# A decode block on one core: head 27's rows of wo by eight small loads on partitions 0 to 63, LN2's sums on the vector engine, one filler product fewer

## The chip, the core and the metric

The kernel runs on one core of a Trainium2 chip, as one program from the first load to the last store. The metric is the device time of one execution in microseconds (us). Beside the timed runs there is one profiled execution; its span is the time between its first and its last instruction, and its own time is a little longer. All profile lines come from that execution, and times in them count from the start of its span.

## What is computed

One decode step (one new token, batch 2) of a transformer block with adaptive layer norm: attention over the last 4096 positions of a key and a value cache (32 query heads on 8 key-value heads, head size 128), then a feed-forward block with SiLU. Everything is float32. The model size D is 512 and the hidden size F is 1792.

```
mod = silu(c) @ w_mod                      # six vectors per batch row
h   = layernorm(x) * (1 + ca) + sa
o   = softmax(q k^T / sqrt(128)) v         # q = h @ wq, last 4096 keys and values
x   = x + ga * (o @ wo)                    # wo: 4096 x 512, 32 heads of 128 rows
h   = layernorm(x) * (1 + cb) + sb         # LN2
x   = x + gb * (silu(h @ w1) @ w2)
```

The inputs are 97.5 MB, of which the keys and values are 67 MB, wo is 8 MB, w1 and w2 are 3.7 MB each.

## The kernel before

**Loads.** All weights and caches go through one buffer of eight slots of 16 KB on each of the 128 partitions (`slots`, RING = 8), filled in turn (`stream`, L72). SP issues these loads in program order: w_mod, x, wq, then keys and values of four groups in turn (`load_group`, L79), then wo, w1 and w2 (`load_runs`, L85). SP is one queue of instructions: a load that has to wait holds back all that SP issues later. wo comes in two loads (`load_wo`, L359): heads 0 to 23 in slots 0 to 2 and heads 24 to 31 in slot 3. Both are issued as soon as the last group's scores are done with the key slots, about 10 us before their data can move, since the last values stand ahead of them in the DMA queues. w1 follows in two loads, w2 in five.

**Semaphores.** Each load that SP or ACT issues reports its landing on one of eight semaphores, DMAHW0 to DMAHW7, which the program gives out in turn: the load of c, from ACT, has 0, x has 1, wq 2, the first keys 3, the first values 4, and so on; the fourth values have 2, wo's heads 0 to 23 have 3, and heads 24 to 31 have 4. A load that takes a semaphore for a second time gets a wait for the load that had it last, unless SP has waited for that one already.

**Work.** Four groups (batch row times half of the heads) run one after the other. Each has scores on TensorE (`scores`, L274), a softmax (`softmax`, L290), the weighted sum of the values (`weighted`, L319), and a turn of the result by products with a small identity (`collect`, L335: four products `oT`, L345, each of which gives 128 x 4, and a copy into `oTn`, L353, where a head q has the 32 columns `oTn[:, q, :]`).

**The tail.** After the last group TensorE multiplies `oTn` of each head with its rows of wo (`acc_o`, L413: 32 products), ACT and TensorE turn that sum (`gather`, L392), DVE adds the residual (`x1T`), and LN2 runs with its columns on partitions: `column_means` (L439) sums over partitions by four products with the matrix `mean512` for the mean, and again by four for the variance, between the second and the third quarter of the product with w1 (`hid`, L459). Then SiLU, the product with w2 (`acc_yw`, L489, and `yx`, L501), a last DVE step (L522) and the store (L523).

**Fillers.** `busy(n, ...)` (L263) issues n products whose result nothing reads; there are four of them ahead of the 32 products with wo.

In float32 each product of the program is two passes of TensorE, so the profile counts twice as many matmuls as the text here.

Of the kernel before, what the change touches and what calls it, by code (L numbers as in the profile page):

```python
# [8 lines left out]
F32 = mybir.dt.float32  # L9
AF = mybir.ActivationFunctionType  # L10
ALU = mybir.AluOpType
AX = mybir.AxisListType

P = 128
B, D = 2, 512
HQ, HKV, DH = 32, 8, 128
G = HQ // HKV
F = 1792
EPS = 1e-5
RING = 8  # L20


def first_load(slots):
# [5 lines left out]
def adaln_block(  # L29
# [4 lines left out]
    v_cache: bass.AP,  # L34
    wq: bass.AP,
    wo: bass.AP,
    w1: bass.AP,
    w2: bass.AP,
    c: bass.AP,
# [13 lines left out]
    nc = tc.nc  # L53
# [5 lines left out]
    once = ctx.enter_context(tc.tile_pool(name="once", bufs=1))  # L59
# [25 lines left out]
    def load_runs(w, per, lo, hi):  # L85

        e = w.shape[1]
        n = -(-(hi - lo) * e // 4096)
        t = stream(n)[:, : (hi - lo) * e].rearrange("p (q e) -> p q e", e=e)
        inorder(nc.sync.dma_start(t, w.rearrange("(p q) e -> p q e", q=per)[:, lo:hi, :]))  # L90
        return t
# [23 lines left out]
    mean512 = const([P, P], "mean512")  # L115
# [19 lines left out]
    qs = const([P, 4 * 256 + 64], "qs")  # L135
    nc.gpsimd.memset(qs, 0.0)  # L136
    rowsum = const([P, 4], "rowsum")

    oTn = const([P, 32, 32], "oTn")
    nc.gpsimd.memset(oTn, 0.0)  # L140
    hT, uT = const([P, 4, 32], "hT_b"), const([P, F // P, 32], "uT")
    nc.gpsimd.memset(hT, 0.0)
# [8 lines left out]
    inorder = tc.keep_in_program_order  # L151
# [106 lines left out]
    vt = {0: load_group(v_cache, 0)}  # L258
    stat = lambda grp, v, s: qs[:, 256 * grp + 64 * v + 32 * s : 256 * grp + 64 * v + 32 * s + 32]

    oT = bank("O", "oT")[:, :64]
    STEPS = 4
    def busy(n, unread):  # L263

        for _ in range(n):
            inorder(nc.tensor.matmul(  # L266
                unread[0:32, :],
                id4,
                warm,
                start=True,  # L270
                stop=True,
            ))
# [62 lines left out]
    def collect(grp, o_ps, rl):  # L335

        o_sb = once.tile([P, 4 * DH], F32, tag="wide", name=f"ob{grp}")
        for c in (slice(0, D // 2), slice(D // 2, D)):
            nc.scalar.activation(o_sb[:, c], o_ps[:, c], AF.Copy, scale=rl)  # L339
        last = grp == STEPS - 1  # L340
        if last:
            busy(1, junk[0])
        cols = oT[:, 16 * grp : 16 * grp + 16]
        for v in range(4):
            inorder(nc.tensor.matmul(  # L345
                cols[:, 4 * v : 4 * v + 4],
                o_sb[:, v * DH : (v + 1) * DH],
                id4[:, 4 * v : 4 * v + 4],
                start=True,
                stop=True,  # L350
            ))
        b, n = divmod(grp, 2)
        (nc.vector.tensor_copy if last else nc.scalar.copy)(  # L353
            oTn[:, 16 * n : 16 * n + 16, 16 * b], cols
        )

    wot, junk = [], []

    def load_wo(lo, hi):  # L359
        wt = load_runs(wo, 32, lo, hi)  # L360
        wot.extend(wt[:, q, :] for q in range(hi - lo))

    for grp in range(STEPS):
        s_ps = scores(grp)
        if grp < STEPS - 1:
            kt[grp + 1] = load_group(k_cache, grp + 1)
        else:
            load_wo(0, 24)
            load_wo(24, 32)
        rl = softmax(grp, s_ps)  # L370
        o_ps = weighted(grp)
        if grp == STEPS - 1:
            junk.append(bank("C", "junk0"))
        if grp < STEPS - 1:
            vt[grp + 1] = load_group(v_cache, grp + 1)
        collect(grp, o_ps, rl)
# [30 lines left out]

    acc = bank("D", "acc_o")
    ao = bank("A", "ao")[:, :P]
    busy(4, junk[0])  # L410
    for q in range(32):
        g = q % 4
        inorder(nc.tensor.matmul(  # L413
            acc[32 * g : 32 * g + 32, :],
            oTn[:, q, :],
            wot[q],
            start=(q < 4),
            stop=(q >= 28),
        ))
    gather(ao, acc, "acc_o_sb", True, True, fill=1)  # L420
    busy(1, junk[1])
# [16 lines left out]

    def column_means(t, name):  # L439

        m = bank("B", name)[:, :B]
        for k in range(4):
            inorder(nc.tensor.matmul(m, mean512, t[:, k, :], start=(k == 0), stop=(k == 3)))
        return m

    mean = column_means(x1T, "mean_b")
    busy(1, junk[1])
    dT = once.tile([P, 4, B], F32, tag="dT", name="dT")
    nc.vector.tensor_sub(dT, x1T, mean[:, None, :].to_broadcast([P, 4, B]))
# [2 lines left out]
    )  # L452
    sq = once.tile([P, 4, B], F32, tag="sq", name="sq")
    nc.vector.tensor_mul(sq, dT, dT)
    FC = F // 4
    hp = bank("A", "hid")[:, :FC]
    for k in range(4):
        for g in range(4):
            inorder(nc.tensor.matmul(  # L459
                hp[32 * g : 32 * g + 32, :],  # L460
                hT[:, k, :],
                w1t[k][:, g * FC : (g + 1) * FC],
                start=(k == 0),
                stop=(k == 3),
            ))
        if k == 1:
            var = column_means(sq, "var_b")
            std = once.tile([P, B], F32, tag="stdb", name="std_b")
            nc.scalar.activation(std, var, AF.Sqrt, bias=eps_t)
            rstd = once.tile([P, B], F32, tag="rstdb", name="rstd_b")  # L470
            nc.vector.reciprocal(rstd, std)
# [53 lines left out]
    tc.no_tile_sem_insts.add(store.ins.name)  # L525


_INS = ["A_x", "A_k_cache", "A_v_cache", "A_wq", "A_wo", "B_w1", "B_w2", "c", "w_mod"]


# [59 lines left out]
```

## Time and profile before

| | |
|---|---|
| time, median of 3 runs | 233.1 us (233.04 to 233.44) |
| the profiled execution: its own time, its span | 233.04 us, 231.4 us |
| TensorE (PE) busy | 126.8 us (55%) |
| PE weight loads (PEld) | 45.9 us (20%) |
| VectorE (DVE), ScalarE (ACT), GpSimd (POOL) busy | 15.0, 19.7, 7.7 us |
| granted TensorE clock, mean | 0.80 |
| moved by DMA | 97.65 MB, 422 GB/s over the span |

A line of the profile's groups names the program line, the engine, the operation and the tiles (out<-in). SPq is SP's queue; "DMA slots<-in_A_wo_dram" is the landing of a load of wo into the slots. A chain of waits lists what the last instruction waited for, followed back to the start. In the rows of the stages, "(x20)" counts instructions and PEclk is the granted clock of TensorE, 1.00 for full speed. w1 and w2 are named in_B_w in the trace, since numbers in names are left out.

### The profile page before, as it was taken

The numbers are of one execution on the slowest core, as the hardware profiler recorded it, in microseconds if no ns is written. First come the engines' busy times: TensorE is split into PE (matmuls) and PEld (weight loads), VectorE is DVE, ScalarE is ACT, GpSimd is POOL, SyncE is SP. The second block draws the span as 40 slices with busy tenths as digits, with TensorE's granted clock in tenths as the row PEclk, the third lists the DMA queues.
The fourth block names the chain that finished last, engine by engine and source line by source line (L and its number), as shares of the span: only waits on it lengthen the run. The fifth ranks groups of instructions, "written<-read, shape, count | busy, mean of one in ns | idle before, by whom it ended". The sixth has DMA issues, their size and how long they took to land.

```text
span 231.4 us, 2188 instructions
## 1 busy us (share of the span) xinstructions
PE 126.8 (55%) x982; PEld 45.9 (20%) x982; DVE 15.0 (6%) x44; ACT 19.7 (9%) x45; POOL 7.7 (3%) x28
## 2 busy tenths in 40 slices
PE   0005906831950781491096078139509607999986
PEld 0003301310210221121033012112202202345333
DVE  0004020000011000002000000100000200000130
ACT  0203010110040010001001000100100100000331
POOL 8102000000000000000000000000000000000000
PEclk9999995985796596598579659656957965999999
DMA  9998988989889898898999989999899999999993
GB/s 399 417 454 362 544 362 385 513 374 532 362 374 532 374 513 374 385 513 385 487 396 396 510 385 467 408 408 498 385 430 445 419 456 408 416 405 442 413 411 137
DMA packets 2915, 97.65 MB, mean 422 GB/s; under 512 B 460, under 2 KB 476, under 8 KB 1116
## 3 DMA queue, kind: packets, MB, share of 16 engines
q1 hardware_dynamic: 2748, 97.52, 97.9%
q8 instruction: 7, 0.11, 0.2%
q10 hardware_dynamic: 160, 0.01, 0.0%
HBM read 97.53 MB, written 0.01 MB: 421 GB/s over the span
## 4 chain that ended last, share of the span: by engine, by line
DMA 73%; PE 23%; POOL 2%; issue 1%; SPq 0%; ACT 0%; DVE 0%; POOLq 0%
DMA slots<-in_A_v_cache_dram 50%; PE o L326 16%; DMA slots<-in_A_wq_dram 13%; DMA slots<-in_B_w_dram 10%; PE q L235 4%; PE acc_yw L489 1%; PE yx L501 1%; PE qT L245 0%; POOL qs L136 0%; POOL oTn L140 0%; SPq L152 0%; ACT q_sb L243 0%; POOL warm L114 0%; POOL avg L104 0%; POOL same L108 0%
## 5 line engine op out<-in xcount | busy, mean ns | idle before, releaser
L326 PE MATMUL o<-slots,probs 128*32 128x512 f32 x256 | 37.9, 755 | 29.1 <-DMA slots<-in_A_v_cache_dram 29.1
L281 PE MATMUL s<-slots,qs 128*32 128x512 f32 x256 | 35.5, 718 | 32.3 <-DMA slots<-in_A_k_cache_dram 32.3
L326 PEld LDWEIGHTS o<-slots,probs 128*32 128x32 f32 x256 | 11.5, 131 | 52.2 <-issue 52.2
L281 PEld LDWEIGHTS s<-slots,qs 128*32 128x32 f32 x256 | 9.4, 130 | 55.2 <-issue 39.0
L235 PE MATMUL q<-slots,hq_T 128*32 128x512 f32 x64 | 9.2, 724 | 7.3 <-DMA slots<-in_A_wq_dram 7.3
L293 DVE TENSOR_REDUCE mx<-s 128x1 f32<-128x512 f32 x4 | 2.8, 691 | 140.5 <-PE s L281 140.5
L173 PE MATMUL mean_a<-mv_a,avg 128*128 128x1 f32 x2 | 0.6, 347 | 18.4 <-DVE mv_a L170 18.4
L266 PE MATMUL junk<-warm,id 128*32 128x512 f32 x20 | 9.6, 595 | 0.0
L339 ACT ACTIVATE ob<-o,rl 128x256 f32<-128x256 f32 x8 | 3.4, 470 | 69.4 <-PE o L326 69.4
L413 PE MATMUL acc_o<-slots,oTn 128*32 128x512 f32 x64 | 7.2, 593 | 0.0
L295 ACT ACTIVATE mp<-part,mx 128x8 f32<-128x8 f32 x4 | 1.2, 300 | 70.0 <-DVE mx L293 70.0
L209 PE MATMUL m_sp<-slots,scT 128*32 128x512 f32 x32 | 5.9, 827 | 0.0
L345 PE MATMUL oT<-id,ob 128*128 128x4 f32 x32 | 4.2, 255 | 1.9 <-ACT ob L339 1.9
L235 PEld LDWEIGHTS q<-slots,hq_T 128*32 128x32 f32 x64 | 2.3, 130 | 13.3 <-issue 13.2
L345 PEld LDWEIGHTS oT<-id,ob 128*128 128x128 f32 x32 | 3.9, 191 | 5.5 <-ACT ob L339 5.5
L308 PE MATMUL lp<-rowsum,same 128*128 128x1 f32 x8 | 1.7, 286 | 5.1 <-ACT pr L303 5.1
L206 PE MATMUL m_a<-slots,scT 128*32 128x256 f32 x32 | 3.6, 543 | 1.1 <-POOL scT L163 1.1
L413 PEld LDWEIGHTS acc_o<-slots,oTn 128*32 128x32 f32 x64 | 3.6, 110 | 3.3 <-issue 3.1
L173 PEld LDWEIGHTS mean_a<-mv_a,avg 128*128 128x128 f32 x2 | 0.5, 310 | 18.4 <-issue 18.4
L297 PE MATMUL mg<-mp,same 128*128 128x8 f32 x8 | 1.6, 266 | 4.6 <-ACT mp L295 4.6
L459 PE MATMUL hid<-slots,hT_b 128*32 128x448 f32 x32 | 3.4, 544 | 0.0
L489 PE MATMUL acc_yw<-slots,uT 128*32 128x512 f32 x22 | 2.8, 599 | 0.9 <-DMA slots<-in_B_w_dram 0.9
(95 smaller groups left out, 59.9 us busy)
## 6 DMA issues: line engine op xcount, KB each, us to landing
slots<-in_w_mod_dram SPq DMA_DIRECT2D x1, 6144.0 KB, 17.1
slots<-in_A_wo_dram SPq DMA_DIRECT2D x1, 6144.0 KB, 25.6
slots<-in_B_w_dram SPq DMA_DIRECT2D x1, 2688.0 KB, 17.8
slots<-in_A_wo_dram SPq DMA_DIRECT2D x1, 2048.0 KB, 29.6
slots<-in_B_w_dram SPq DMA_DIRECT2D x1, 2048.0 KB, 23.1
slots<-in_B_w_dram SPq DMA_DIRECT2D x1, 896.0 KB, 19.6
slots<-in_B_w_dram SPq DMA_DIRECT2D x1, 768.0 KB
slots<-in_B_w_dram SPq DMA_DIRECT2D x3, 256.0 KB, 16.0
```

The source lines that it names most:

```text
L206: nc.tensor.matmul(m_a[r, :], scT[:, k, :], ab[:, g], start=(k == 0), stop=(k == 3))
L209: nc.tensor.matmul(m_sp[r, :], scT[:, k, :], cd[:, g], start=(k == 0), stop=(k == 3))
L235: inorder(nc.tensor.matmul(q_ps[32 * g : 32 * g + 32, :], hq_T[:, k, :], wqt[:, k, lo : lo + 4 * DH], start=(k == 0), stop=(k == 3),))
L266: inorder(nc.tensor.matmul(unread[0:32, :], id4, warm, start=True, stop=True,))
L281: inorder(nc.tensor.matmul(s_ps[32 * c : 32 * c + 32, :], stat(grp, v, s), kt[grp][:, lo : lo + 512], start=(s == 0 and v == 0), stop=(s = ...
L293: nc.vector.tensor_reduce(mx, s_ps, axis=AX.X, op=ALU.max)
L326: inorder(nc.tensor.matmul(o_ps[r : r + 32, :], probs[grp % 2][:, 32 * n + 16 * s : 32 * n + 16 * s + 32], vt[grp][:, lo : lo + 512], star ...
L339: nc.scalar.activation(o_sb[:, c], o_ps[:, c], AF.Copy, scale=rl)
L345: inorder(nc.tensor.matmul(cols[:, 4 * v : 4 * v + 4], o_sb[:, v * DH : (v + 1) * DH], id4[:, 4 * v : 4 * v + 4], start=True, stop=True,))
L413: inorder(nc.tensor.matmul(acc[32 * g : 32 * g + 32, :], oTn[:, q, :], wot[q], start=(q < 4), stop=(q >= 28),))
L459: inorder(nc.tensor.matmul(hp[32 * g : 32 * g + 32, :], hT[:, k, :], w1t[k][:, g * FC : (g + 1) * FC], start=(k == 0), stop=(k == 3),))
L489: inorder(nc.tensor.matmul(yw[32 * g : 32 * g + 32, :], uT[:, tt, :], w2t[tt], start=(tt < 4), stop=(tt >= WIDE - 4),))
```

## The change

Head 27's rows of wo no longer come with the other heads. On the host wo is packed as 31 heads, and head 27's 128 rows of 512 are packed as `wo2`, 8 x 8 x 1024. In the kernel they go to a tile of their own, `woh`, on partitions 0 to 63 with two rows each: partition p's two rows belong to row positions p and p + 64 of the head. Eight loads of eight partitions each bring them (partitions p, p + 4, ..., p + 28 for one p), 32 KB each, 4 KB a partition. They are issued by SP between the two loads of wo, the second of which is shorter by one head (3584 instead of 4096 elements a partition).

```diff
+    woh = const([P // 2, 2, D], "woh")
-    oTn = const([P, 32, 32], "oTn")
+    oTn = const([P, 33, 32], "oTn")
...
             load_wo(0, 24)
-            load_wo(24, 32)
+            for i in range(8):
+                p = 32 * (i // 4) + i % 4
+                inorder(nc.sync.dma_start(
+                    woh[p : p + 29 : 4, :, :].rearrange("p s e -> p (s e)"), wo2[i]
+                ))
+            load_wo(24, HQ - 1)
```

Since the two halves of head 27 now stand on the same 64 partitions, its 32 columns are needed twice: as before, of which partitions 0 to 63 are read, and once more with the upper half moved down, in a 33rd place of `oTn`. One more turning product of one column does that in groups 1 and 3, and the copy into `oTn` there has 17 columns.

```diff
+        if n:
+            v = SPLIT % 16 // 4
+            inorder(nc.tensor.matmul(
+                cols[:, 16:17],
+                o_sb[:, v * DH + DH // 2 : v * DH + DH // 2 + DH],
+                id4[:, SPLIT % 16 : SPLIT % 16 + 1],
+                start=True,
+                stop=True,
+            ))
...
-    busy(4, junk[0])
-    for q in range(32):
+    busy(3, junk[0])
+    heads = [q for q in range(HQ) if q != SPLIT]
+    parts = [(oTn[:, q, :], wot[i]) for i, q in enumerate(heads)]
+    parts[24:24] = [(oTn[: P // 2, q, :], woh[:, i, :]) for i, q in enumerate((SPLIT, HQ))]
+    for i, (o, w) in enumerate(parts):
```

LN2's means are taken over the four column blocks first, by one reduction on DVE, and then over the partitions by one product instead of four:

```diff
     def column_means(t, name):
+        ks = once.tile([P, B], F32, tag=f"ks_{name}", name=f"ks_{name}")
+        nc.vector.tensor_reduce(ks, t.rearrange("p k b -> p b k"), axis=AX.X, op=ALU.add)
         m = bank("B", name)[:, :B]
-        for k in range(4):
-            inorder(nc.tensor.matmul(m, mean512, t[:, k, :], start=(k == 0), stop=(k == 3)))
-        return m
+        return m, lambda: inorder(nc.tensor.matmul(m, mean512, ks, start=True, stop=True))
```

What stands in the program. On SP, before, from the fourth load of values (the last group's) to w2's first, with the semaphores that each waits for (PE_51 stands for the products that free its slots):

```order
L82 DMA slots<-in_A_v_cache_dram 128x16384 [waits DMAHW0_51,PE_51]
L90 DMA slots<-in_A_wo_dram 128x12288 [waits DMAHW1_51,PE_51]
L90 DMA slots<-in_A_wo_dram 128x4096 [waits PE_51]
L90 DMA slots<-in_B_w_dram 128x5376 [waits DMAHW2_51,PE_51]
L90 DMA slots<-in_B_w_dram 128x1792
L90 DMA slots<-in_B_w_dram 128x4096 [waits PE_51]
```

The same place on SP in the changed program:

```order
L84 DMA slots<-in_A_v_cache_dram 128x16384 [waits DMAHW0_51,PE_51]
L92 DMA slots<-in_A_wo_dram 128x12288 [waits DMAHW1_51,PE_51]
L384 DMA woh<-in_A_wo_dram 8x1024 x6
L384 DMA woh<-in_A_wo_dram 8x1024 [waits DMAHW2_51]
L384 DMA woh<-in_A_wo_dram 8x1024 [waits DMAHW3_51]
L92 DMA slots<-in_A_wo_dram 128x3584 [waits DMAHW4_51,PE_51]
L92 DMA slots<-in_B_w_dram 128x5376 [waits DMAHW5_51,PE_51]
L92 DMA slots<-in_B_w_dram 128x1792 [waits DMAHW6_51]
L92 DMA slots<-in_B_w_dram 128x4096 [waits DMAHW7_51,PE_51]
```

Eight loads came in ahead of wo's second load, and with them one full turn of the eight semaphores: the small loads take 4, 5, 6, 7, 0, 1, 2 and 3. The seventh waits for the fourth values (semaphore 2), and the eighth for wo's heads 0 to 23 (semaphore 3). wo's second load and all of w1 and w2 stand behind it.

On TensorE, before, from the turning products of the last group to the first filler after the products with wo (junk_591 and junk_607 are written by fillers):

```order
L345 MATMUL oT<-id,ob_592 128x4 x4
L266 MATMUL junk_591<-warm,id 32x512 x4
L413 MATMUL acc_o<-slots,oTn 32x512 x32
L266 MATMUL junk_607<-warm,id 32x512
L400 MATMUL ao<-acc_o_sb,id 32x128 x4
L266 MATMUL junk_607<-warm,id 32x512
L443 MATMUL mean_b<-x1T,mean_87 128x2 x4
```

The same place in the changed program:

```order
L350 MATMUL oT<-id,ob_602 128x4 x4
L359 MATMUL oT<-id,ob_602 128x1
L269 MATMUL junk_601<-warm,id 32x512 x3
L434 MATMUL acc_o<-slots,oTn 32x512 x24
L434 MATMUL acc_o<-woh,oTn 32x512 x2
L434 MATMUL acc_o<-slots,oTn 32x512 x7
L269 MATMUL junk_618<-warm,id 32x512
L418 MATMUL ao<-acc_o_sb,id 32x128 x4
L269 MATMUL junk_618<-warm,id 32x512
L465 MATMUL mean_b<-ks_mean_b,mean_87 128x2
```

There is one turning product more, one filler fewer, 33 products with wo instead of 32 with the two of head 27 after the first 24, and one product for the mean instead of four.

More of the change, by code (lines that the diff above doesn't have):

```diff
@@ L20 @@
 RING = 8
+SPLIT = 27
 def first_load(slots):
@@ L36, in adaln_block @@
     wo: bass.AP,
+    wo2: bass.AP,
     w1: bass.AP,
@@ L259, in adaln_block @@
     stat = lambda grp, v, s: qs[:, 256 * grp + 64 * v + 32 * s : 256 * grp + 64 * v + 32 * s + 32]
-    oT = bank("O", "oT")[:, :64]
+    oT = bank("O", "oT")[:, :68]
     STEPS = 4
@@ L342, in collect @@
             busy(1, junk[0])
-        cols = oT[:, 16 * grp : 16 * grp + 16]
+        b, n = divmod(grp, 2)
+        per = 16 + n
+        cols = oT[:, 17 * grp : 17 * grp + per]
         for v in range(4):
@@ L351, in collect @@
             ))
-        b, n = divmod(grp, 2)
+        if n:
[7 more added lines that the diff above has]
+            ))
         (nc.vector.tensor_copy if last else nc.scalar.copy)(
-            oTn[:, 16 * n : 16 * n + 16, 16 * b], cols
+            oTn[:, 16 * n : 16 * n + per, 16 * b], cols
         )
@@ L359, in load_wo @@
     def load_wo(lo, hi):
-        wt = load_runs(wo, 32, lo, hi)
+        wt = load_runs(wo, HQ - 1, lo, hi)
         wot.extend(wt[:, q, :] for q in range(hi - lo))
@@ L409, in adaln_block @@
     ao = bank("A", "ao")[:, :P]
-    busy(4, junk[0])
-    for q in range(32):
-        g = q % 4
+    busy(3, junk[0])
[3 more added lines that the diff above has]
+    for i, (o, w) in enumerate(parts):
+        g = i % 4
         inorder(nc.tensor.matmul(
             acc[32 * g : 32 * g + 32, :],
[L415 to L418, printed above, removed]
+            o,
+            w,
+            start=(i < 4),
+            stop=(i >= len(parts) - 4),
         ))
@@ L439, in column_means @@
     def column_means(t, name):
+        ks = once.tile([P, B], F32, tag=f"ks_{name}", name=f"ks_{name}")
+        nc.vector.tensor_reduce(ks, t.rearrange("p k b -> p b k"), axis=AX.X, op=ALU.add)
         m = bank("B", name)[:, :B]
-        for k in range(4):
-            inorder(nc.tensor.matmul(m, mean512, t[:, k, :], start=(k == 0), stop=(k == 3)))
-        return m
-    mean = column_means(x1T, "mean_b")
+        return m, lambda: inorder(nc.tensor.matmul(m, mean512, ks, start=True, stop=True))
+    mean, product = column_means(x1T, "mean_b")
+    product()
     busy(1, junk[1])
@@ L454, in adaln_block @@
     nc.vector.tensor_mul(sq, dT, dT)
+    var, product = column_means(sq, "var_b")
     FC = F // 4
@@ L466, in adaln_block @@
         if k == 1:
-            var = column_means(sq, "var_b")
+            product()
             std = once.tile([P, B], F32, tag="stdb", name="std_b")
@@ L525, in adaln_block @@
     tc.no_tile_sem_insts.add(store.ins.name)
-_INS = ["A_x", "A_k_cache", "A_v_cache", "A_wq", "A_wo", "B_w1", "B_w2", "c", "w_mod"]
+_INS = ["A_x", "A_k_cache", "A_v_cache", "A_wq", "A_wo", "A_wo2", "B_w1", "B_w2", "c", "w_mod"]
 def kernel(**inputs):
@@ L536 @@
     from concourse.bass_utils import run_bass_kernel_spmd as _run
-    inputs = {name: _np.asarray(inputs[name]) for name in _INS}
+    inputs = {name: _np.asarray(inputs[name]) for name in _INS if name in inputs}
     for name, order in (("A_k_cache", "keys"), ("A_v_cache", "values")):
@@ L550 @@
     inputs["B_w2"] = inputs["B_w2"].reshape(F, P, 4).transpose(0, 2, 1).reshape(F, D)
-    inputs["A_wo"] = inputs["A_wo"].reshape(HQ, DH, D).transpose(1, 0, 2).reshape(HQ * DH, D)
+    a = inputs["A_wo"].reshape(HQ, DH, D)
+    inputs["A_wo"] = _np.delete(a, SPLIT, axis=0).transpose(1, 0, 2).reshape((HQ - 1) * DH, D)
+    a = a[SPLIT].reshape(2, 2, 8, 4, D).transpose(1, 3, 2, 0, 4)
+    inputs["A_wo2"] = a.reshape(8, 8, 2 * D)
     arrays = {f"in_{name}_dram": _np.ascontiguousarray(inputs[name]) for name in _INS}
```

## The prediction

> **What bounds the kernel now.** The page comes first: the slices of the span, the DMA queues, and the chain that ended last.
>
> ```profile
> span 231.4 us, 2188 instructions
> DMA  9998988989889898898999989999899999999993
> q1 hardware_dynamic: 2748, 97.52, 97.9%
> q8 instruction: 7, 0.11, 0.2%
> DMA 73%; PE 23%; POOL 2%; issue 1%; SPq 0%; ACT 0%; DVE 0%; POOLq 0%
> ```
>
> The DMA engines are busy from end to end: queue q1, which carries SP's loads, fills 97.9% of the span of 16 engines. Time can be saved only by moving fewer bytes, by ending the engines more evenly, or behind the last load. Time is lost wherever the queues run dry. The chain in order of time shows how the loads follow each other:
>
> ```profile
> 7.25 29.18 DMA slots<-in_A_wq_dram
> ...
> 47.47 28.94 DMA slots<-in_A_v_cache_dram
> ...
> 86.09 29.12 DMA slots<-in_A_v_cache_dram
> ...
> 124.27 29.59 DMA slots<-in_A_v_cache_dram
> ...
> 164.07 28.40 DMA slots<-in_A_v_cache_dram
> ...
> 202.15 23.05 DMA slots<-in_B_w_dram
> 225.20 0.14 issue
> 225.34 2.82 PE acc_yw L489 x22
> 228.16 1.56 PE yx L501 x91
> ```
>
> Start and duration give the landings: the last values at 164.07 + 28.40 = 192.47, w2's first load at 225.20. The tail is tight on both sides, since DVE ends `uT`, which the same products need, at 224.93 + 0.20 = 225.13 (its row stands below): the work between the products with wo and those with w2 has almost no slack against the loads.
>
> The change is decided by SP's queue, so these views come next: SP's instructions in order of time, its waits, and the loads with their time from issue to landing.
>
> ```profile
> 0.00 0.36 SPq L576 DMA_DIRECT2D slots<-in_w_mod_dram  x1
> 6.51 0.67 SPq L152 DMA_DIRECT2D xc<-in_A_x_dram  x1
> ...
> 181.35 1.19 SPq L90 DMA_DIRECT2D slots<-in_A_wo_dram  x2
> 200.38 13.40 SPq L90 DMA_DIRECT2D slots<-in_B_w_dram  x7
> ```
>
> ```profile
> SPq L90 <- DMA slots<-in_A_wo_dram: 4.5, 1, 4.5
> ```
>
> ```profile
> slots<-in_w_mod_dram SPq DMA_DIRECT2D x1, 6144.0 KB, 17.1
> slots<-in_A_wo_dram SPq DMA_DIRECT2D x1, 6144.0 KB, 25.6
> ...
> slots<-in_A_wo_dram SPq DMA_DIRECT2D x1, 2048.0 KB, 29.6
> ...
> out_dram<-yo ACTq DMA_DIRECT2D x1, 8.0 KB, 1.4
> ```
>
> wo's heads 0 to 23, issued at 181.35, land at 181.35 + 25.6 = 206.95. Its second load is issued 0.86 later (1.19 less one issue of about 0.33), at 182.21, and lands at 211.8. So 6144 KB take 206.95 - 192.47 = 14.48 us behind other loads, and 2048 KB take 4.85. Before, SP waited 4.5 us for the first of them with nothing urgent behind it: w1 and most of w2's bytes had been issued.
>
> **The change part by part.**
>
> *The wait.* The new order on SP (shown with the change) has the eighth small load wait for wo's heads 0 to 23, because it takes their semaphore again. SP is one queue, so wo's second load and all of w1 and w2 stand behind that wait, until 206.95. By then nothing is left in the DMA queues: the last engine has just ended the load waited for, and seven small loads of 4 KB a partition are short (2048 KB are 16 KB a partition and 128 KB an engine in 4.85 us; seven rows of 4 KB are 28 KB, about 1.1 us on the engines that carry them, while the others are idle).
>
> *The restart.* From 206.95 SP issues the eighth small load (0.33 to 0.67, by a wide load and by x's of eight partitions; I take 0.5) and, after some 0.1 for its waits, wo's second load at about 207.55. From an issue on empty queues to landing, over the time of the bytes, there are two ends. w_mod, the only wide load on empty queues, took 17.1 where the same 6144 KB take 14.48 behind others: 2.6. The store took 1.4 in all, for 8 KB. I take 2.4, near w_mod's since it is the same kind of load; a lower value stays possible because it is the first of the program. Now 1792 KB are left of 2048: 4.85 x 7/8 = 4.24. Landing: 207.55 + 2.4 + 4.24 = 214.2, where it was 211.8. **+2.4 us** for this load and all behind it, which follow with the same bytes as before. The 0.6 us that the lighter load saves is in it.
>
> *Unevenness of the engines.* Queue q8, of kind instruction, has 7 packets. These are its rows for the stretches 36.4 to 76.4, 76.5 to 115.2 and 207 to 212:
>
> ```profile
> q8 instruction: 1, 0.02, 0.1%
> ...
> q8 instruction: 2, 0.03, 0.3%
> ...
> q8 instruction: 1, 0.02, 1.2%
> ```
>
> The last row is 1.2% of 16 x 5 us, so one packet holds one engine for 1 us. A load has landed when its slowest engine is done, and the chain shows the price: from wq's landing (36.43) to the first values' (76.41) are 39.98 us for two loads of one size, while the next such pairs take 38.80, 38.65 and 38.61. The first packet cost 1.3; the later ones cost nothing, if they hit other engines, none of which was then later than the first. The empty queues after 206.95 end this cover: all engines start anew together. The packet at 207 to 212 comes while TensorE is in its products with wo, which still start at 207.1, so it now falls on wo's second load, and whichever engine it hits is the last one from there on. **+1.3 us** (0 if it comes while the queues are empty). All later loads then land 3.7 later; w2's first at 228.9.
>
> *TensorE and its clock.* These rows are from the timeline of PE and DVE, and then from the stages:
>
> ```profile
> 207.09 7.19 PE L413 MATMUL acc_o<-slots,oTn 128*32 128x512 f32 x64
> 214.12 1.02 PE L266 MATMUL junk<-warm,id 128*32 128x512 f32 x2
> 216.36 1.05 PE L443 MATMUL mean_b<-x1T,mean 128*128 128x2 f32 x8
> 218.36 1.71 PE L459 MATMUL hid<-slots,hT_b 128*32 128x448 f32 x16
> 220.00 1.05 PE L443 MATMUL var_b<-sq,mean 128*128 128x2 f32 x8
> 224.93 0.20 DVE L163 TENSOR_TENSOR uT<-z,sgh 128x28 f32<-128x28 f32 x1
> ```
>
> ```profile
> 142.80:146.21 3.41, 1.65 (x14) 1.00 0.90 384
> 146.21:149.63 3.42, 0.59 (x2) 0.50 1.24 537
> 173.52:176.93 3.41, 3.41 (x20) 0.50 1.15 500
> 176.93:180.35 3.42, 3.42 (x37) 1.00 0.91 388
> 180.35:183.76 3.41, 2.19 (x22) 1.00 1.20 519
> 183.76:187.17 3.41, 0.38 (x2) 1.00 0.80 346
> ```
>
> A product with wo takes 7.19/32 = 0.22. After 24 of them and head 27's two TensorE stands at 212.8 and waits for wo's second load until 215.5 (214.2 + 1.3): 2.7 us. The stages show what that does to the granted clock. A stretch of 3.41 us with 1.65 busy is followed by half clock, one with 2.19 busy is not, and at half clock 20 passes fill the time of 37. A gap of 2.7 us leaves less than 1.8 busy in the stretch that holds most of it, so half clock follows for one stretch or more, somewhere between the last seven products with wo and those with w2. At full clock the chain has room. It ends its products with wo at 215.5 + 7 x 0.22 = 217.0 against 214.3, 2.7 later, while the loads are 3.7 later: 1.0 of room ahead of w1's landing, and 0.6 more by the shorter mean (below). Behind w1's landing the room is 0.1 (225.13 against 225.20) and 0.8 by the shorter variance. At half clock, with 1 - 20/37 = 46% less done in a stretch, one stretch of 3.41 us loses 1.6. The seven products (1.5 us at full clock) lie in the first room. The 16 with w1 (1.71 for each eight) can lose up to 2.9 and the eleven with w2 up to 2.1, less the second room of 0.9: from 0 to about 2.5 shows at the end, by where the stretches fall. I take one stretch over that room, 1.6 - 0.9: **+0.7**.
>
> The Trainium skill, "TensorE: Matmul & The Clock Gate", Part 1, has the clock fall after at least one idle window of about 3.4 us. By that rule a gap of 2.7 us would leave it full and this term 0. The rows of 142.80 and 146.21 differ: a stretch that was half busy was enough; the measurement decides.
>
> *The small edits.* One filler fewer (0.22) shortens nothing, as the products with wo wait for the landing at 206.95 anyway. The two turning products (priced like one of the mean, 1.05/4 = 0.26) lie where TensorE waits for loads or runs fillers. The 33rd product is ahead of the gap. Three products of four fewer in each of mean and variance save 0.8 each of 1.05; a DVE reduction of few elements adds about 0.2 (DVE's smallest steps take 0.17 to 0.20), for the variance beside TensorE's first products with w1. That is 0.6 and 0.8 less, in a stretch that waits for w1: it is the room above, and nothing of it reaches the end by itself. If the loads did not bound the tail, it would be worth these 1.4.
>
> **Sum.** 2.4 + 1.3 + 0.7 = 4.4 on the execution's own 233.04: 237.4. The median of the runs shown is 233.1, the same within a tenth.
>
> **Rivals.**
>
> *No stop.* If the eighth load's wait let the queues stay filled, head 27's 256 KB would only be spread otherwise: 16 KB (4.85/8 = 0.6 us) less on the engines that leave the small loads alone, and as much more on those that carry them. Were the late engines all of the first kind, each load would land 0.6 sooner, and the tail would follow by LN2's savings: 232.4, on the other side. Were one late engine of the other kind, the loads would land up to 0.6 later, 233.1 to 233.6. The point from which it decides: wo's second load must be issued before the engines run dry, about 3 us (0.6 and 2.4) before 206.95. The wait in SP's order speaks against it: 4% and 3%. The Trainium skill, "DMA: Bandwidth & Descriptors", "Why a DMA increments its semaphore by 16 and not by 1" and "The descriptor swizzle", has a load of eight partitions run on the lowest eight engines, and these serve partitions 0 to 63 in a wide load; no row here shows which engines are late.
>
> *A cheap restart.* The stop comes, but with a lag near the store's 1.4, no q8 packet on the path and full clock: 233.04 + 1.4, to 2.4 with w_mod's lag: 234.4 to 235.4. The packet's time is tied to TensorE's progress, which does not change ahead of the stop: 13%.
>
> *Half clock to the end.* TensorE stays slow through w1 and w2: 2.5 instead of 0.7, 239.2. Fillers and waits in the tail are sized for loads that come earlier, which speaks for it; the full stretch of hid's products speaks against: 15%.
>
> **How the numbers follow.** The forecast, 236.0 to 238.4, has 65%. The range for 8 in 10 takes in most of the cheap restart above and half clock below 239.2: 235.0 to 239.2. Outside are the rival without a stop (7%), the cheap half of the cheap restart (7%) and a part of the half clock (6%). Faster by over 0.2% (about what a measurement of this kernel can tell from no change) is the first half of the first rival, 4%; its other half counts as within 0.2%, 3%; the rest, 13 + 15 + 65, is slower: 93%.
>
> **What would show it.** In the changed profile SP's waits name a landing of wo ahead of the small loads, with about 14 us; the slices of DMA show a hole near 207 to 209, where it had none; wo's second load lands near 214 to 215.5 with an issue near 207.5; PE waits for it after 26 products with wo; the clock is half in some stretch after 214; the chain still ends in w2's loads or in the work behind hid. If the second load is issued before 190 and there is no hole, the forecast is wrong in its first step.

## The result, and the profile after

| | before | after |
|---|---|---|
| time, median of 4 runs | 233.12 us (233.04 to 233.44) | 236.01 us (235.88 to 236.35) |
| the profiled execution: own time, span | 233.04 us, 231.4 us | 236.35 us, 234.5 us |
| ratio of the times | | 1.0124, 95% interval 1.0106 to 1.0141 |

The change makes the kernel slower by 2.9 us in the median. The profiled execution of the changed kernel is the slowest of its four, 3.3 us over the profiled one of before. These lines are from the changed kernel's page: its span, the busy share of the DMA engines in 40 slices, and the queue that carries SP's loads.

```profile
span 234.5 us, 2189 instructions
DMA  9998989899898999989899999999999999949994
q1 hardware_dynamic: 2876, 97.52, 96.9%
```

The 36th slice (205.2 to 211.1 us) is new: a 4 among nines. Before, no slice but the last was under 8. The queue moved the same 97.52 MB in a longer span, 96.9% of it instead of 97.9%. This view is SP's timeline over the place of the change (start, duration, line, tiles, count), and the next one lists what SP waited for there (total, times, longest):

```profile
182.67 0.33 SPq L92 DMA_DIRECT2D slots<-in_A_wo_dram  x1
183.05 24.73 SPq L384 DMA_DIRECT2D woh<-in_A_wo_dram  x8
207.88 0.38 SPq L92 DMA_DIRECT2D slots<-in_A_wo_dram  x1
208.36 7.78 SPq L92 DMA_DIRECT2D slots<-in_B_w_dram  x7
```

```profile
SPq L384 <- DMA slots<-in_A_wo_dram: 13.9, 1, 13.9
SPq L384 <- DMA slots<-in_A_v_cache_dram: 5.5, 1, 5.5
```

The eight small loads hold SP for 24.73 us: the seventh waits for the fourth values (5.5), the eighth for wo's heads 0 to 23 (13.9). wo's second load was issued at 182.21 before; now it is issued at 207.88, after the first has landed. The chain of waits, from its last 52 us, shows the way to the end:

```profile
182.67 24.46 DMA slots<-in_A_wo_dram
...
210.22 18.03 DMA slots<-in_B_w_dram
228.38 2.86 PE acc_yw L512 x22
231.24 1.56 PE yx L524 x91
```

wo's first load lands at 207.14 (0.2 later than before), but w2's first at 210.22 + 18.03 = 228.25, where it was 225.20: 3.05 later, and what stands behind it takes as long as before. TensorE's timeline shows whether the gap also cost something there (in brackets the idle time ahead of the row and what ended it):

```profile
207.27 5.36 PE L434 MATMUL acc_o<-slots,oTn 128*32 128x512 f32 x48 [0.88 <-DMA slots<-in_A_wo_dram]
212.56 1.05 PE L434 MATMUL acc_o<-woh,oTn 64*32 64x512 f32 x4
214.74 1.92 PE L434 MATMUL acc_o<-slots,oTn 128*32 128x512 f32 x14 [1.13 <-DMA slots<-in_A_wo_dram]
...
221.41 1.71 PE L482 MATMUL hid<-slots,hT_b 128*32 128x448 f32 x16 [1.15 <-DMA slots<-in_B_w_dram]
...
228.38 2.86 PE L512 MATMUL acc_yw<-slots,uT 128*32 128x512 f32 x22 [1.61 <-DMA slots<-in_B_w_dram]
```

```profile
213.55:216.96 3.41, 2.28 (x18) 1.00 0.99 425
216.96:220.40 3.44, 2.99 (x16) 1.00 0.98 417
220.40:223.80 3.40, 2.39 (x26) 1.00 1.05 446
```

The second fence is the table of stretches (length, PE busy, instructions, granted clock, DMA share, GB/s). TensorE waits 1.13 for wo's second load, and the clock stays at 1.00. It then waits for loads again, ahead of the products with w1 and with w2, so in this execution the loads set the end.

The records of the landings give the time at which each of the 16 engines ended wo's second load. It is the base of much that follows:

```
before   eleven engines 210.10 to 210.37, five engines 211.31 to 211.78
after    sixteen engines 214.17 to 214.69
```

Before, five engines ran 0.9 to 1.7 us behind the others, and the last of them set the landing. After the stop all start anew, and the 16 end within 0.5.

### The profile page after: what moved, and what is told of

Its sections match the earlier page's. It is cut to its first block, busy times and chain, and to the rows that moved or that the text cites. A ratio compares the mean times of both kernels' runs of the same rounds, so it can differ in the third digit from the quotient of the medians.

```text
span 234.5 us, 2189 instructions
## 1 busy us (share of the span) xinstructions
PE 129.2 (55%) x974; PEld 44.3 (19%) x974; DVE 15.4 (7%) x46; ACT 19.7 (8%) x45; POOL 7.7 (3%) x28
## 3 DMA queue, kind: packets, MB, share of 16 engines
q1 hardware_dynamic: 2876, 97.52, 96.9%
## 4 chain that ended last, share of the span: by engine, by line
DMA 72%; PE 22%; POOL 3%; DVE 1%; SPq 1%; issue 1%; ACT 0%; DVEq 0%; POOLq 0%
DMA slots<-in_A_k_cache_dram 49%; PE s L284 16%; DMA slots<-in_A_wo_dram 10%; DMA slots<-in_B_w_dram 8%; DMA xc<-in_A_x_dram 5%; PE m_sp L212 2%; PE acc_yw L512 1%; PE m_a L209 1%; SPq L92 1%; PE yx L524 1%; PE acc_o L434 0%; DVE sgc L165 0%; POOL qs L138 0%; POOL oTn L143 0%; POOL sgc L162 0%
## 5 line engine op out<-in xcount | busy, mean ns | idle before, releaser
L284 PE MATMUL s<-slots,qs 128*32 128x512 f32 x256 | 38.1, 763 | 31.1 <-DMA slots<-in_A_k_cache_dram 31.1
L329 PE MATMUL o<-slots,probs 128*32 128x512 f32 x256 | 37.2, 744 | 25.9 <-DMA slots<-in_A_v_cache_dram 25.9
L238 PE MATMUL q<-slots,hq_T 128*32 128x512 f32 x64 | 10.2, 794 | 8.0 <-DMA slots<-in_A_wq_dram 8.0
L269 PE MATMUL junk<-warm,id 128*32 128x512 f32 x18 | 8.8, 595 | 0.0
L434 PEld LDWEIGHTS acc_o<-slots,oTn 128*32 128x32 f32 x62 | 2.2, 110 | 7.1 <-issue 3.3
## 6 DMA issues: line engine op xcount, KB each, us to landing
slots<-in_w_mod_dram SPq DMA_DIRECT2D x1, 6144.0 KB, 17.5
```

The lines of the kernel that those rows point to most:

```text
L238: inorder(nc.tensor.matmul(q_ps[32 * g : 32 * g + 32, :], hq_T[:, k, :], wqt[:, k, lo : lo + 4 * DH], start=(k == 0), stop=(k == 3),))
L269: inorder(nc.tensor.matmul(unread[0:32, :], id4, warm, start=True, stop=True,))
L284: inorder(nc.tensor.matmul(s_ps[32 * c : 32 * c + 32, :], stat(grp, v, s), kt[grp][:, lo : lo + 512], start=(s == 0 and v == 0), stop=(s = ...
L329: inorder(nc.tensor.matmul(o_ps[r : r + 32, :], probs[grp % 2][:, 32 * n + 16 * s : 32 * n + 16 * s + 32], vt[grp][:, lo : lo + 512], star ...
L434: inorder(nc.tensor.matmul(acc[32 * g : 32 * g + 32, :], o, w, start=(i < 4), stop=(i >= len(parts) - 4),))
```

## Experiments

The theory: the eighth small load's turn of the semaphores stops SP until wo's first load has landed, the DMA queues run dry, and this restart is all that the change costs. The rivals: the loss comes from the small loads themselves (partly filled engines, short rows), or from TensorE (33rd product, new LN2). Each kernel was timed against the kernel before on the same chip, whose medians were 233.17 to 233.21.

### The stop alone: unread small loads in the kernel before

```diff
+    unread8 = [const([4 * B, P], f"unread{i}") for i in range(8)]
...
             load_wo(0, 24)
+            for t in unread8:
+                inorder(nc.sync.dma_start(t, c))
             load_wo(24, 32)
```

> The kernel before, with eight loads of c's 4 KB into tiles that nothing reads, issued between wo's two loads; no head is split, LN2 and the fillers are as before. By the theory the turn of the eight semaphores alone makes the stop: SP waits until about 207, the second load of wo (2048 KB here, 0.6 us more than the changed kernel's) is issued near 208 and lands near 215.3, 3.5 us later than before, and the time is 236.2 to 237.2, or 1.3 more if the q8 packet falls on that load. By the rival (the split of head 27 or the LN2 edit costs) it is within 0.3 us of 233.1.

Measured: 236.75 us (236.21 to 237.02), ratio 1.0141 (1.0121 to 1.016). SP's timeline and waits in this kernel:

```profile
181.38 26.19 SPq L371 DMA_DIRECT2D unread<-in_c_dram  x8
207.67 0.35 SPq L90 DMA_DIRECT2D slots<-in_A_wo_dram  x1
```

```profile
SPq L371 <- DMA slots<-in_A_wo_dram: 14.3, 1, 14.3
```

Eight loads of 4 KB each, 32 KB in all, which nothing reads, cost more than the whole change: 3.5 us, with the same issue (207.67) and the same kind of wait. wo's second load, here the full 2048 KB, landed at 215.63, its last engine 0.5 behind the next (215.09). The layout of head 27, its products and LN2 are not needed for the loss.

### The change without the stop: four small loads on each side

```diff
         else:
+            load_small(0, 4)
             load_wo(0, 24)
-            for i in range(8):
-                ...
+            load_small(4, 8)
             load_wo(24, HQ - 1)
```

> The changed kernel with four of its eight small loads issued ahead of wo's first load and four behind it; everything else as changed. By the theory (the time went into the stop of SP's queue until wo's heads 0 to 23 had landed, and the restart of empty DMA queues) no wait ends later than about 193 us, the hole in the DMA slices near 207 to 209 is gone, wo's second load lands by 211.8, and the time falls to between 232.3 and 233.0, by whether the engines that carry the small loads are the early ones (232.4) or not (233.0 and more). By the rival (the small loads themselves, their 4 KB rows or the other split over the engines, or the changed work on TensorE and DVE, are what costs) the time stays between 235.5 and 236.3.

Measured: 233.58 us (232.66 to 233.79, 12 runs), ratio 1.0007 (0.9996 to 1.0019). The slices of its DMA engines, its timeline of SP and its chain:

```profile
DMA  9998988989989899898999989999999999989994
```

```profile
181.86 11.86 SPq L379 DMA_DIRECT2D woh<-in_A_wo_dram  x4
193.82 0.38 SPq L92 DMA_DIRECT2D slots<-in_A_wo_dram  x1
```

```profile
181.49 25.41 DMA slots<-in_A_wo_dram
...
206.96 17.77 DMA slots<-in_B_w_dram
```

Everything of the change is in it, except that four of the eight loads now stand ahead of wo's first. SP now waits for the fourth values only, wo's second load is issued at 193.82, 13 us ahead of the first one's landing, and no slice ahead of the last is under 8. In the profiled execution (232.84) w2's first load lands at 206.96 + 17.77, about 224.74, 0.5 sooner than before. The stop is the loss; without it the ratio's interval takes in 1, and the change cannot be told from the kernel before. Its runs fall into two groups, 232.66 to 232.95 (3 of 12) and 233.38 to 233.79 (9), which is taken up below.

### LN2's sums alone

The edit is the LN2 part of the change, made in the kernel before.

```diff
+        nc.vector.tensor_reduce(ks, t.rearrange("p k b -> p b k"), axis=AX.X, op=ALU.add)
...
-        for k in range(4):
-            inorder(nc.tensor.matmul(m, mean512, t[:, k, :], start=(k == 0), stop=(k == 3)))
...
+        return m, lambda: inorder(nc.tensor.matmul(m, mean512, ks, start=True, stop=True))
```

> The kernel before with the LN2 sums on the vector engine alone. By the theory the loads bound the tail: the product with w2 waits for its first load at 225.2 whatever LN2 takes, uT comes 0.7 to 1.4 us earlier, and the time is within 0.2 us of 233.1. By the rival (the work between wo and w2 bounds the tail as well) it falls by 0.5 to 1.4, to 231.7 to 232.6.

Measured: 233.36 us (233.15 to 233.57, 12 runs), ratio 1.0005 (0.9996 to 1.0013). Its timeline of DVE and its chain:

```profile
224.44 0.20 DVE L163 TENSOR_TENSOR uT<-z,sgh 128x28 f32<-128x28 f32 x1
```

```profile
201.11 24.27 DMA slots<-in_B_w_dram
```

`uT` is ready at 224.64, 0.5 sooner than before (225.13), and the products with w2 go on waiting for their load, until 201.11 + 24.27, about 225.4. What an engine saves ahead of a wait for a load does not reach the end here.

### All eight small loads ahead of wo

```diff
         else:
-            load_wo(0, 24)
             for i in range(8):
                 ...
+            load_wo(0, 24)
             load_wo(24, HQ - 1)
```

> The changed kernel with all eight small loads issued ahead of wo's first load instead of behind it. The eighth then takes the semaphore of the fourth values. By the theory SP stops there until the values have landed near 192.5, the DMA queues run dry at that place instead of at 207, wo's first load is issued near 193.3 and everything from it on lands 2.5 to 3 us later than in the kernel before; a q8 packet that comes in TensorE's products with wo now falls on full queues and costs up to 1.3 more: 235.7 to 237.4, with the hole in the DMA slices near 193. By the rival (what costs is the place of the small loads between wo's two loads, or head 27's products) the time goes back to 233.0 to 233.8.

Measured: 237.93 us (237.71 to 238.68), ratio 1.021 (1.0195 to 1.0225), above what was expected. The chain and two rows of TensorE's timeline:

```profile
162.88 29.46 DMA slots<-in_A_v_cache_dram
...
192.36 0.62 SPq L383
...
193.08 17.13 DMA slots<-in_A_wo_dram
210.35 10.77 PE acc_o L434 x66
...
230.68 2.78 PE acc_yw L512 x22
```

```profile
210.35 7.95 PE L434 MATMUL acc_o<-slots,oTn 128*32 128x512 f32 x48 [4.77 <-DMA slots<-in_A_wo_dram]
```

The stop moves with the wait: now it stands behind the fourth values (192.34). The price of a restart can be read again: wo's first load takes 17.13 from issue to landing, 2.65 more than the 14.48 that its bytes take behind other loads, so it lands 3.26 later than before. Two things come on top. One engine ended wo's second load at 215.91, the next one at 214.47. And TensorE, which waited 4.77, ran the 48 passes with wo in 7.95 instead of 5.36, at half clock (0.50 from 208.8 to 215.6). From there the chain is work, not loads: the products with w2 start at 230.68, while w2's first load landed at 229.09.

### Four loads of 16 partitions in the same place

The host packs head 27's rows as 4 x 16 x 1024; everything else is as in the changed kernel.

```diff
-            for i in range(8):
-                p = 32 * (i // 4) + i % 4
+            for i in range(4):
                 inorder(nc.sync.dma_start(
-                    woh[p : p + 29 : 4, :, :].rearrange("p s e -> p (s e)"), wo2[i]
+                    woh[i : i + 61 : 4, :, :].rearrange("p s e -> p (s e)"), wo2[i]
```

> The changed kernel with head 27's rows brought by four loads of sixteen partitions instead of eight loads of eight, at the same place between wo's two loads; same bytes, same tile, all other edits kept. Four loads do not turn the eight semaphores once, so by the theory nothing waits, wo's second load is issued before 190 and the time is 233.0 to 233.5. Sixteen partitions spread over all engines, so a late engine costs the same whichever it is, and the twelve times should not fall in two groups 0.6 apart as with four loads ahead and four behind. By the rival (small loads at this place, or head 27's products of 64 partitions, cost the 2.9) it stays between 235.5 and 236.3.

Measured: 234.51 us (234.2 to 237.47, 8 runs), ratio 1.0074 (1.0043 to 1.0106): the stop is gone, but about 1 us more than expected is left. Its timeline of SP and its chain:

```profile
181.56 2.48 SPq L383 DMA_DIRECT2D woh<-in_A_wo_dram  x4
184.08 0.58 SPq L92 DMA_DIRECT2D slots<-in_A_wo_dram  x1
```

```profile
181.18 26.34 DMA slots<-in_A_wo_dram
...
207.58 18.58 DMA slots<-in_B_w_dram
```

Four loads take four semaphores, SP passes at once (184.08), and the queues stay full. But wo's first load lands at 181.18 + 26.34 = 207.52 (before 206.95), and w2's first at 207.58 + 18.58 = 226.16 (225.20). The packet records show why, up to a point: from about 205.4 to 208.5 the rows of every load take longer. The last rows of wo's first load, 48 KB each, take 2.16 to 2.28 us instead of 1.815, those of its second load, 14 KB each, 0.56 to 0.99 instead of 0.535, and of the 64 rows of 4 KB the first 35 take 0.159 and the later ones up to 0.316. The small rows stand behind wo's first load on each engine, so their own length cannot have held that load up. In the kernel with four small loads on each side no such stretch exists: the rows of wo's second load take 0.535 there, and 62 of the 64 small rows 0.159. What slows all rows here stays open, and so does the one run of 237.47 (the next is 235.02). So this shape of the small loads costs about 1.3 us over the kernel before (233.17) without any stop.

### The two terms that did not show: packets of the queue "instruction" and half clock

The prediction expected a packet of queue q8 (kind instruction) to make one engine late after the stop, and half clock after TensorE's gap. The changed kernel shows hardly anything of the first and nothing of the second. To tell whether they are real, two kernels move these packets in time, by unread products at TensorE's start. The first adds 51 full ones:

```diff
+    early = bank("C", "early")
+    for _ in range(51):
+        inorder(nc.tensor.matmul(early[0:32, :], id4, warm, start=True, stop=True))
```

> The changed kernel with 51 unread products on TensorE at the very start, where TensorE waits for w_mod: about 204 instructions more, so that each q8 packet comes that many of TensorE's instructions sooner in the program, and the one that came at 231.0 in the changed kernel should come near 209 to 214. By the theory of the uneven engines it then falls on wo's second load just after the restart, one engine is 1.3 us later than the rest from there on, and the time is 237.0 to 237.6, more where the longer gap of TensorE brings half clock. By the rival (a q8 packet after the restart costs nothing) it stays between 235.8 and 236.3.

Measured: 272.8 us (272.26 to 274.66), ratio 1.1705 (1.1672 to 1.1739). Nearly all of that has nothing to do with the question, as its chain near the start shows:

```profile
17.52 45.78 PE early L161 x101
```

TensorE does not start before w_mod has landed (17.5), and such a product takes 0.9 us (45.78 for 101 passes), so the kernel lost 40 us ahead of the first group, and its time cannot be held against the expectation. Its tail can. The first row is from TensorE's timeline there, the other two are stretches:

```profile
251.55 3.40 PE L438 MATMUL acc_o<-slots,oTn 128*32 128x512 f32 x14 [1.95 <-DMA slots<-in_A_wo_dram]
247.76:251.17 3.41, 1.84 (x13) 1.00 1.05 448
251.17:254.58 3.41, 3.03 (x14) 0.50 0.98 423
```

The stop is there as before (SP waits 13.8 for wo's first load), and the packet came at 244.31, 1.2 behind that load's landing (243.13), as in the changed kernel (208.31 and 207.14). So here too a packet stands in the hole, at the same distance from the stop. But here one engine ended wo's second load at 251.51, 0.9 behind the next (250.61), and stayed as far behind in the loads after it. TensorE waited 1.95, and half clock followed for one stretch. It did not reach the end: the products with w2 wait for their load again, which lands 21.76 after wo's first load, against 21.11 in the changed kernel.

The second kernel adds small products, which cost little:

```diff
+    early = bank("C", "early")
+    for _ in range(32):
+        inorder(nc.tensor.matmul(early[0:32, :2], id4, warm[:, :2], start=True, stop=True))
```

> The changed kernel with 32 unread products of two columns at TensorE's start (about 3 us, where it waits for the condition vector anyway): 128 instructions more, so that a q8 packet comes about half a period from its place in the changed kernel, near 215 to 222 instead of 208.3, on full queues behind the restart. By the theory of the uneven engines it makes one engine late for all loads from there on, by 0.9 to 1.4 against 0.3 in the changed kernel: 236.6 to 237.4. By the rival (q8 packets do not decide the last landing) 235.8 to 236.3.

Measured: 238.27 us (238.12 to 238.49), ratio 1.0218 (1.0204 to 1.0233); 2.3 above the changed kernel and above what was expected. The first fence is the view of DMA queues of this kernel for 217 to 219 us, the second of the changed kernel for 207 to 210; then come a row of TensorE's timeline and two of its stretches in this kernel.

```profile
q8 instruction: 1, 0.02, 2.9%
```

```profile
q8 instruction: 1, 0.02, 1.8%
```

```profile
222.08 2.80 PE L486 MATMUL hid<-slots,hT_b 128*32 128x448 f32 x16 [2.41 <-DMA slots<-in_B_w_dram]
```

```profile
219.14:222.55 3.41, 1.00 (x10) 1.00 0.99 418
222.55:225.97 3.42, 3.42 (x22) 0.50 1.05 449
```

Here a packet comes at 217.7, when the queues are full again. 2.9% of 16 engines for 2 us is 0.93 us of one engine, and that engine is late from there on: w1's first load is ended by 15 engines at 220.09 to 220.45 and by the last at 221.94, 1.5 behind. TensorE therefore waits 2.41, and the stretch with 1.00 of 3.41 busy is followed by one at 0.50, in which hid's products take 2.80 instead of 1.71. The products with w2 then start at 229.84, 0.9 after w2's first load landed (228.92). Both terms are real, with about the sizes of the prediction (1.3 and 0.7). They are not all of the 2.3: the store at the end takes longer, by this line from the issues of this kernel, where the changed kernel has 1.4.

```profile
out_dram<-yo ACTq DMA_DIRECT2D x1, 8.0 KB, 2.4
```

Fifteen of its engines end at 235.68 to 235.84 and one at 236.82, and another packet of q8 runs from 234.81 to 235.74. Without that 1.0 the time would be about 237.3, by estimate, inside the expectation.

In the changed kernel the packet came at 208.3, in the hole (1.8% of 16 engines for 3 us is 0.86 of one engine), and held up little. Seven engines ended the eighth small load at 209.14 to 209.27 and one at 210.36; wo's second load shows no engine apart (214.63 and 214.69), and w2's first only just (228.01 and 228.25). A packet in the hole is not always that cheap. In the kernel with the unread small loads one came at 208.53 and took 1.8, and one engine was 0.5 behind from wo's second load on; with the 51 full products it was 0.9. In the kernel with the small products, where no packet came in the hole, all 16 engines ended wo's second load within 0.34 (213.75 to 214.09). The records do not name the engine of a packet or of a landing, so that the late engine is the packet's is argued from these four kernels.

The Trainium skill, "TensorE: Matmul & The Clock Gate", Part 1, has the clock fall after an idle window of about 3.4 us. This trace differs: a gap of 2.41 in a stretch that was 0.29 busy was enough. So was one of 1.95 in a stretch that was 0.54 busy (1.84 of 3.41, with the 51 products), while 0.67 busy (2.28 of 3.41, in the changed kernel) was not followed by half clock. But the busy share of a stretch does not decide it alone, as a row and two stretches of the kernel with the unread small loads show:

```profile
215.67 1.92 PE L416 MATMUL acc_o<-slots,oTn 128*32 128x512 f32 x16 [2.89 <-DMA slots<-in_A_wo_dram]
213.67:217.08 3.41, 1.41 (x16) 1.00 1.07 458
217.08:220.49 3.41, 3.26 (x28) 1.00 0.95 410
```

There TensorE waited 2.89 for wo's second load, longer than the 2.7 of the prediction; the stretch was 0.41 busy, and the clock stayed full. Over all profiles of this case, a stretch of 3.41 us at full clock with under 1.4 us busy was followed by half clock each time (72), one with over 2.6 never (226), and in between both happened (29 of 72 by half clock).

### What is left without the stop

The kernel with four small loads on each side was profiled once more, to see one run of its slower group:

> The kernel with four small loads ahead of wo's first load and four behind it once more, for a second profile, since its twelve times fell in two groups (232.7 to 233.0, and 233.4 to 233.8). By the theory that the group depends on which engines the q8 packets hit, a profile of the upper group has a late engine among the eight that carry the small loads, and one of the lower group, like the first, has none.

Measured: 233.52, a run of the slower group. Its chain:

```profile
206.76 18.70 DMA slots<-in_B_w_dram
```

wo's first load lands no later than in the other execution (206.70 against 206.90), but w2's first at 206.76 + 18.70 = 225.46 instead of 224.74. The landings of w2's last load show one engine apart:

```
execution of 232.84   last 228.50, next 228.26
execution of 233.52   last 229.15, next 228.55
```

The packet of queue q8 comes at 210.85 in the one and at 211.02 in the other. By the order of the landings it falls on an engine that carries no small loads in the first execution, and on one that does in the second. By this reading the gain of 0.5 is there when the packet hits an engine with few bytes, and lost when it hits one with many. These are two executions; that the same holds for all runs of the two groups is argued from them, not shown. The Trainium skill, "DMA: Bandwidth & Descriptors", "Why a DMA increments its semaphore by 16 and not by 1", has a load of eight partitions run on the eight lowest-numbered engines. The landings agree as far as they go, without numbers of engines: each small load's data end on eight engines, by their order other ones than the five that were late before.

The last kernel takes back LN2's sums in that kernel (four products each for mean and variance, as before the change):

```diff
-        nc.vector.tensor_reduce(ks, t.rearrange("p k b -> p b k"), axis=AX.X, op=ALU.add)
...
+        for k in range(4):
+            inorder(nc.tensor.matmul(m, mean512, t[:, k, :], start=(k == 0), stop=(k == 3)))
```

> The kernel with four small loads ahead of wo's first load and four behind it, with the LN2 sums of the kernel before (four products each). By the theory the loads bound the tail and LN2's products hide behind w1 and w2: within 0.3 us of the same kernel with the new sums, 233.2 to 233.9 in the median. By the rival (the new sums are worth 0.5 or more once the loads are not held up) 234.0 to 234.6.

Measured: 234.35 us (233.48 to 235.16, 6 runs), ratio 1.0053 (1.0034 to 1.0071): 0.8 slower in the median than with the new sums, against the main expectation. The profiled execution is the fastest of the six (233.48). A row of its chain and one of TensorE's timeline:

```profile
206.93 8.19 PE acc_o L438 x66
```

```profile
225.82 2.77 PE L514 MATMUL acc_yw<-slots,uT 128*32 128x512 f32 x22 [0.80 <-DVE uT L166]
```

The end of this chain is work, not a load: TensorE waits for `uT` (225.77), while w2's first load landed at 225.46. The products with wo last until 206.93 + 8.19 = 215.12, where they ended at 214.3 before, mainly since head 27's two products of 64 partitions take 1.0 us. The new sums pay for that. In this layout they are worth 0.8 by the medians, though they are worth nothing alone; this execution shows 0.3 of it, and where the rest goes in the slower ones is not shown.

## Why the prediction was right, and which sizes were off

237.4 was predicted, with 235.0 to 239.2; 236.01 was measured. The direction and the mechanism are as predicted: SP's waits name wo's first load with 13.9 (about 14 was named), the hole lies in the slice of 205 to 211 (near 207 to 209 was named), wo's second load was issued at 207.88 (207.55) and landed at 214.69 (214 to 215.5), and the chain ends in w2's loads. The unread loads in the kernel before show that the turn of the semaphores alone does it; in the split kernel all the rest of the change together cannot be told from nothing (0.9996 to 1.0019). The sizes were less right: of 4.4 us forecast 2.9 came, two of the three terms stayed away, and that 236.01 still falls into the forecast's 236.0 to 238.4, at its very edge, is luck. The wider range held because the rival of a cheap restart had been let into it. Point by point:

- **The restart, +2.4, was 2.9.** wo's first load landed 0.2 later (207.14). From there to the issue of the second took 0.74, not 0.6: SP needed 0.62 for the small load, where 0.5 was taken. From issue to landing over the bytes were 214.69 - 207.88 - 4.24 = 2.57; 2.4 was taken, between 1.4 and 2.6. The same sum gives 2.36 with the small unread products, 3.11 with the unread small loads, 3.39 with the 51 products, and 2.65 for wo's first load with all small loads ahead. Up to the last engine but one it is 2.3 to 2.6 in all five, so w_mod's 2.6 was the right end, and what goes beyond it is one late engine. Part of the lag is seen in the rows: in the changed kernel the first of wo's second load start at 208.9, 1.0 behind the issue, and the first eleven take 0.83 to 1.21, where later ones take 0.535.
- **Unevenness, +1.3, was 0.2 or less.** This is the step that was most off. The packet came 2.5 us sooner (208.31) than before (210.81), although TensorE's products with wo started 0.2 later. In the split kernel, which has the same program on TensorE and no hole, it comes at 210.85; so it was an idle DMA engine, as far as these runs tell, that served it sooner. It fell into the hole, the case that the prediction put at 0. That price is roughly right for this execution: from wo's second load (2.9 later) to w2's first (3.05 later) the loss grows by 0.15, and one engine ends w2's first load 0.24 behind the next. It is not right in general, as the 0.5 and 0.9 of the two kernels above show. In the kernels where the packet fell on full queues behind a stop, it made one engine late by 1.4 and 1.5.
- **Half clock, +0.7, was 0.** The gap of 2.7 was to lie between 212.8 and 215.5. It was 1.13: the load landed at 214.69, as the packet didn't hold it up, and head 27's products ended at 212.56 + 1.05 = 213.61 instead of 212.8, since products of 64 partitions cost 1.0 and not 0.44. The third term hangs on the second, as its 215.5 is 214.2 + 1.3; without the packet the prediction's own gap is 1.4. And the step from the gap to the clock was too firm: a gap of 2.89 with 1.41 busy, in the kernel with the unread small loads, left the clock full, while gaps of 1.95 and 2.41 halved it.
- **The small edits at nothing: right.** LN2 alone is worth nothing (233.36), and `uT` is ready at 227.50, ahead of the load at 228.25. The price of a filler was wrong, though: 0.22 was taken from the products with wo, and a filler takes 0.9. It hid behind the same load.
- **Rivals.** No stop: refuted. Cheap restart: its clock was right, and nearly so its packet, but its lag (1.4 to 2.4) was too low. Half clock to the end: half clock came in three other kernels (237.93, 238.27 and 272.8), for a stretch or two, and not in this one. Its price of 2.5 is less than the prediction's own parts, 2.9 + 2.1 - 0.9 = 4.1; no run tests it.

With 0 for the second and third term the restart alone gives 233.04 + 2.9 = 235.9, near the median of 236.01. The profiled execution, at 236.35, is 0.4 above that: 0.15 came between wo's second load and w2's first, and the rest is not followed up here.

## What to carry to other kernels

Count the loads between two large ones on a queue: where completion semaphores are given out in turn, a small load that takes the semaphore of a large one still on its way stops the whole queue, however small it is. Put small loads so that what they wait for lands while enough bytes still stand in the queue. With four on each side of the large load SP waited too, until the fourth values landed at 192.41, but wo's first load with its 14.5 us stood queued behind them: 233.6 instead of 236.0. A hole in a full queue costs the time from landing to next issue and the lag of the first load after it (0.74 and 2.57 here), plus, by chance of place, whatever makes one engine late from there on.

## What the runs showed of the hardware

- An instruction packet of 16 KB holds one DMA engine for 0.9 us (1.8 in one case, in a hole). On full queues behind a stop one engine was then 1.4 to 1.5 us late for every later load; in a hole it was between under 0.1 and 0.9 late. The packet's time is tied to TensorE's progress (with 128 instructions more ahead, the last packets come at 197.6, 217.7 and 234.8 instead of 208.3 and 231.0) and to what else stands in the queues: in the hole it came 2.5 us sooner.
- Half clock followed stretches of 3.41 us with 1.00, 1.65 and 1.84 us busy, and did not follow others with 1.41, 2.19 and 2.28. What decides between 1.4 and 2.6 is open.
- Two float32 products with 64 rows between products with 128 rows took 1.0 us, where two of 128 rows took 0.4.
- Fillers, all of which write the same 32 partitions, took 0.45 us a pass (45.78 for 101), the products with wo 0.11 (5.36 for 48). That the common place in the result is the cause is argued only.
- With four small loads of 16 partitions between two large ones, the rows of all loads slowed for about 3 us (0.56 to 0.99 instead of 0.535 for 14 KB); with loads of eight partitions they did not. The cause is open.
